# Spectral filter and expert layer on one core: another order for the opening loads, for the rest of the first transform, and for the turned loads ahead of the input loads

## The chip, the cores and the metric

The kernel runs on one core of one Trainium2 chip. The metric is the device time of one execution in microseconds (us), as the median of several; lower is better. The profiled execution is a single one, recorded by the hardware profiler, and it took somewhat longer than the runs that are only timed (the table below has both).

## The reference, cut to what matters

```python
def _attn_ref(x, w_r, w_i, b_r, b_i):              # x: (8, 2496, 256)
    X = np.fft.rfft(x, axis=1)
    Xr, Xi = X.real, X.imag
    Yr = Xr @ w_r - Xi @ w_i + b_r
    Yi = Xr @ w_i + Xi @ w_r + b_i
    Yr = np.sign(Yr) * np.maximum(np.abs(Yr) - 0.01, 0.0)
    Yi = np.sign(Yi) * np.maximum(np.abs(Yi) - 0.01, 0.0)
    return np.fft.irfft(Yr + 1j * Yi, n=2496, axis=1)

def _moe_ref(x, w_gate, w1, w2):                   # x: (19968, 256), 8 experts, hidden 1024
    logits = x @ w_gate
    expert_idx = argmax(logits); gate_w = softmax(logits)[expert_idx]
    for e in range(8):
        out[mask_e] = gate_w[mask_e] * (np.maximum(x[mask_e] @ w1[e], 0) @ w2[e])
```

The first function runs on 8 sequences (batches) of 2496 rows, the second on all 19,968 rows together.

## The kernel before, in words

A transform of length 2496 is done as 39 x 64. For each batch `fwd_a` applies the 39-point step: the input lies in six blocks `x` (q = 0 to 5, each loaded by `load_x`; blocks 0 to 4 are 117 x 1024 values, 468 KB, block 5 is 78 x 512 values, 156 KB), and each block is done in one or two pairs (q, g), 11 pairs a batch. The result of a pair (`pa` in PSUM) is copied to SBUF (`ae`, four buffers that are used in turn; for batch 0 most of it into the large tile `z` instead) and stored to a buffer in DRAM (`spec_dram`). `turn` loads it back turned: a tile `t` for slot s of batch b needs rows 12s to 12s+11 of the stored array and is fetched by two transfers of 128 KB. There are 10 slots a batch. In slot s, `fwd_b` multiplies the tile by a block of the basis `bm` (the 64-point step, result `pb`), `halves` copies and splits the result, `mix` multiplies by the weights (`pk`, `pm`, result `v`), `shrink` thresholds it (`r`, `y`), and two slots later `inv_b` goes back (`pv`) by the basis `bi`. Blocks 12 to 19 of `bi` are loaded, blocks 0 to 11 are made on the chip from `bm` by `turn_basis` (four transposes on TensorE into `pi`, one copy on ScalarE).

The program runs a fixed loop of 80 slots (`it`), and the order on each engine is the order of the code; nothing is reordered. Iteration `it` does `fwd_b` of slot it+1, `inv_b` of slot it-2, `mix` of slot it, and what is listed for it of the next batch's first step: ScalarE rounds a block of x (`round_x`, result `xah`), GpSimd takes the remainder (`rest_x`, result `xal`), TensorE multiplies (`fwd_a`), ScalarE copies `ae`, SyncE stores it. Which pair and which load of x belongs to which iteration stands in two tables of offsets (lines 630 to 635). At the end of an iteration come the rounds for the next-but-one iteration, then the basis loads, the turns and the loads of x (lines 709 to 736).

SyncE (SP) issues nearly all transfers, one after the other. When a transfer must wait for data (a turn for the rows that it reads, a load for a buffer to come free), SP waits, and all that stands behind it waits too. Slot k below is the stretch that begins with `pb` of the k-th slot of the loop; slot 10 is the first of batch 1.

Before the loop stands the opening: batch 0's 11 pairs, a store of rows 0 to 47 in pieces (`store_first`), the first turns, a store of rows 48 to 71 and one of rows 72 to 119 (`store_rest`, three transfers each: pair 0's columns from the tile `first_ae`, which is one of the four `ae` buffers, the rest from `z`), blocks of `bm`, and the first two blocks of batch 1. `keep_warm` puts matmuls without use on TensorE while it would have nothing to do. After the spectral part comes the expert layer, in which TensorE has work without a gap; the change doesn't touch it.

Of the kernel before, what the change touches and what calls it, by code (L numbers as in the profile page):

```python
# [24 lines left out]
D = 256  # L25
# [84 lines left out]
class Kernel:  # L110
# [80 lines left out]
    def open_forward(self, st):  # L191
        tc, nc, nb = self.tc, self.nc, self.nb
        f = self.f = self.pool(st, "f", 1, side="right")
        self.xst = ExitStack()
        self.xp = self.pool(self.xst, "xp", 3)
        self.skip(self.xp, 224)
        self.xh, self.xl = {}, {}
        self.tp = self.pool(st, "tp", 6, side="right")
        self.w = self.pool(st, "w", 2, side="right")
        self.psf = self.pool(st, "psf", 1, side="right", space=PSUM)  # L200

        y = [self.w.tile([128, 2, D], F32, tag="y", name=f"first{i}", bufs=3) for i in range(2)]
        self.idle, self.row1, self.brow = y[0][:, 0, :].bitcast(BF16), y[0][0:1, 1, 0:128], y[1][0:1]
        nc.vector.memset(self.idle, 0.0)
        nc.vector.memset(self.row1, 1.0)
        far = f.tile([117, 240], F32, name="far")
        self.far, self.fer = far[:, 0:120], far[0:78, 120:240]
        nc.sync.dma_start(far, self.c_fa)
        self.bm = f.tile([128, K1, 128], F32, name="bm")
        self.bi = f.tile([128, K1, 128], F32, name="bi")  # L210
        self.bias = f.tile([128, 2, D], F32, name="bias")
        self.bias_r = f.tile([128, 2, D], F32R, name="bias_r")
        self.ones = f.tile([128, 128], F32R, name="ones")
        self.xg = {}
        for z, zf in zip(self.zs, self.zf):
            for c in range(2):
                nc.vector.memset(z[:, c, 64:66, :], 0.0)
            nc.vector.memset(zf[:, 5280:5288], 0.0)
        for q in range(6):
            self.load_x(0, q)  # L220
        raw = self.wi.tile([128, 4, D], F32, tag="yb", name="wraw", bufs=4)
        nc.sync.dma_start(raw, self.w_in.rearrange("(c p) n -> p c n", p=128))
        self.skip(self.wi, 160)
        self.raw = {"r": raw[:, 0:2, :], "i": raw[:, 2:4, :]}
        nc.sync.dma_start(self.brow, self.b_in.rearrange("(o h) n -> o h n", o=1))
        self.wh, self.wl = {}, {}
        for nm in "rds":
            self.wh[nm] = f.tile([128, 2, D], F32R, name="wh" + nm)
            self.wl[nm] = f.tile([128, 2, D], F32R, name="wl" + nm)
        self.nlam = f.tile([128, 1], F32, name="nlam")  # L230
        nc.vector.memset(self.nlam, -LAM)
# [138 lines left out]
    def fwd_a(self, b, q, g):  # L370
        nc = self.nc
        x = self.part_x(b, q, g)
        p = self.psi.tile([128, 512], F32, tag="u", name="pa", bufs=4)
        if b:
            h, l = self.xh.pop((b, q, g)), self.xl.pop((b, q, g))
            fh, fl = self.fhl[q == 5]
            for i, (a, v) in enumerate(((fh, h), (fl, h), (fh, l))):
                nc.tensor.matmul(p[:120, :], a, v, start=i == 0, stop=i == 2)
        else:
            nc.tensor.matmul(p[:120, :], (self.far if q < 5 else self.fer)[:x.shape[0], :], x, start=True, stop=True)  # L380
        n = 2 * q + g // 2 - 1
        if b or n < 0:
            ae = self.xp.tile([120, 2, D], F32, tag="ae", name="ae", bufs=4)
            to = ae.rearrange("p g d -> p (g d)")
        else:
            to = self.zs[1][:120, n // 5, 0:NB, :].rearrange("p n a -> p (n a)")[:, n % 5 * 512:n % 5 * 512 + 512]
            ae = to.rearrange("p (g d) -> p g d", g=2)
        if b == 0 and g:
            nc.vector.tensor_copy(to, p[:120, :])
        else:  # L390
            with self.tc.high_priority():
                nc.scalar.copy(to, p[:120, :])
        if b:
            nc.sync.dma_start(self.spec[b % 2][:, 4 * q + g:4 * q + g + 2, :], ae)
        elif n < 0:
            self.first_ae = ae
# [186 lines left out]
    def spectral(self, fwd):  # L583
# [5 lines left out]
        pairs = [(q, g) for q in range(6) for g in ((0, 2) if q < 5 else (0,))]  # L589
        todo = [(b, s) for b in range(nb) for s in range(10)]  # L590
        n = len(todo)
        self.keep_warm(10)
        nc = self.nc
        for i, pair in enumerate(pairs):
            self.fwd_a(0, *pair)
            if i in (0, 5):
                self.store_first(0, 48, *((-1, 0) if i == 0 else (0, 5)))
            if i == 5:
                self.load_basis(0, 4)
            if i in (8, 10):  # L600
                self.store_first(0, 32, *((5, 8) if i == 8 else (8, 10)))
        self.store_first(32, 48, 5, 10)
        self.turn(0, 0, (0,))
# [7 lines left out]
        self.load_basis(8, 12)  # L611
        if nb > 1:
            self.load_x(1, 1)
        self.store_rest(72, 120)
        self.load_basis(12, 16)
        self.keep_warm(6)
        self.spread_bias()
        self.keep_warm(6)
# [9 lines left out]
        for b in range(1, nb):  # L628
            at = 10 * b - 10
            for i, o in enumerate({1: (2, 2, 3, 3, 4, 4, 5, 5, 6, 6, 7), 2: (-2, -1, 0, 1, 1, 2, 3, 4, 4, 5, 6)}.get(  # L630
                    b, (-3, -2, -1, 0, 1, 2, 3, 3, 4, 5, 6))):
                first[at + o].append((b, *pairs[i]))
            for q, o in enumerate({1: (None, None, 0, 1, 2, 3), 2: (-5, -4, -3, -1, 0, 2)}.get(b, (-7, -5, -4, -2, 0, 2))):
                if o is not None:
                    loads[at + o].append((b, q))
        for b in range(nb):
# [4 lines left out]
        for b in range(nb - 1):  # L641
# [5 lines left out]
            for i in range(GH):  # L647
                o = i + 2 if i < 3 else i + 1
                (late if i == 3 else early)[at + o].append((self.inv_z, b, i))
                o = i + 3 if i < 3 else i + 2  # L650
                to = (late if i == 3 else early)[at + o]
                to.insert(0 if i == 2 else len(to), (self.inv_y, b, i))

        for it in range(n):
            b, s = todo[it]
# [53 lines left out]
            for a in first.get(it + 2, ()):  # L709
                if a[0] > 1:  # L710
                    self.round_x(*a)
            if it == 2:
                self.load_basis(16, 20)
            if it in (2, 4):
                self.turn_basis(it // 2)
            if it in (4, 6):
                self.load_inverse(*((12, 16), (16, 20))[it // 2 - 2])
            if not it:
                self.turn(*todo[4])
                self.turn(*todo[5])  # L720
            elif it < 5:
                self.turn(*todo[it + 5])
            for a in loads[it]:
                self.load_x(*a)
            if it in (2, 8, 9):
                self.load_tables(max(it - 7, 0), self.paced)
            if it == 6:
# [2 lines left out]
                self.split_bias(it - 7)  # L730
            if it == 11:
                self.write_blank(self.us[b, s][0:1, 0, 0:1])
            if 6 < it < n - 4:
                if it == 7:
                    self.turn(*todo[it + 3])
                self.turn(*todo[it + 4])
            if b == nb - 3 and s == 6:
                self.tabling = self.table(0)
            if b == nb - 1 and s == 2:
# [586 lines left out]
```

## Time and profile before

| | us |
|---|---|
| median of 3 timed runs (lowest, highest) | 1443.52 (1442.25, 1444.67) |
| the profiled execution | 1455.2 |
| its span in the trace | 1453.3 |
| TensorE matmuls busy in it | 1429.0 |
| VectorE busy | 926.8 |
| ScalarE busy | 770.1 |

The profiled execution is 1.9 us longer than its span, and 11.7 us longer than the median of the timed runs. Differences are worked out inside the trace and applied to the median.

### The profile page before, as it was taken

The page shows a single profiled execution, that of the slowest core. Times are in us where ns is not written, and L with a number is a line of the kernel's source. Part 1 is how long each engine was busy: PE and PEld are TensorE (multiplying, and loading weights), DVE is VectorE, ACT ScalarE, POOL GpSimd, SP SyncE. Part 2 cuts the span into 40 slices and gives each one's busy share as a digit, 9 for nine tenths or more (in the row PEclk, how much of TensorE's full clock was granted, in tenths as well). Part 3 has the DMA queues.
Part 4 walks back from the last instruction along what each step waited for, and adds up shares of the span by engine and source line. Part 5 has one row for each costly group of instructions (what it writes and reads, how often), then busy time and mean ns, then how long its engine had stood idle before and what let it go on. Part 6 is the DMA issues. An engine that isn't in the chain of part 4 may idle for free. (4 is left out here: it accounts for less than half of the span.)

```text
span 1453.3 us, 35136 instructions
## 1 busy us (share of the span) xinstructions
PE 1429.0 (98%) x10521; PEld 1308.2 (90%) x10522; DVE 926.8 (64%) x1960; ACT 770.1 (53%) x1551; POOL 490.8 (34%) x595
## 2 busy tenths in 40 slices
PE   8999999999999989999999999999999999999998
PEld 5889898898989877899999999999999999999997
DVE  4788898988998875555555545454646445446444
ACT  4878787777877763443444434343435334335332
POOL 0452565766674454334311112112112112112111
PEclk9999999999999999999999999999999999999999
DMA  8774565565554232444343323242324224223220
GB/s 236 238 215 133 145 187 161 162 175 164 166 153 151 71 98 72 118 124 111 92 106 105 102 53 107 48 105 66 86 53 105 49 49 107 53 60 89 49 49 29
DMA packets 193212, 161.34 MB, mean 111 GB/s; under 512 B 127163, under 2 KB 163798, under 8 KB 192788
## 3 DMA queue, kind: packets, MB, share of 16 engines
q1 hardware_dynamic: 173043, 114.63, 31.1%
q0 software_dynamic: 19808, 44.03, 8.7%
q8 instruction: 94, 1.54, 0.5%
q14 instruction: 123, 1.00, 0.2%
q10 hardware_dynamic: 144, 0.13, 0.0%
HBM read 241.22 MB, written 66.37 MB: 212 GB/s over the span
## 5 line engine op out<-in xcount | busy, mean ns | idle before, releaser
L1163 PE MATMUL ph<-xh,l 128*128 128x256 f32 x1312 | 363.0, 277 | 0.2 <-DVE l L1094 0.2
L1163 PE MATMUL ph<-xh,h 128*128 128x256 f32 x1312 | 363.1, 277 | 0.0
L1163 PE MATMUL ph<-xl,h 128*128 128x256 f32 x1312 | 362.9, 277 | 0.0
L1203 PE MATMUL po<-h,hh 128*128 128x512 f32 x1296 | 310.5, 390 | 2.3 <-DVEq L1113 1.5
L1169 DVE SCALAR_TENSOR_TENSOR hl<-ph,hh 128x512 fp32r<-128x512 f32 x328 | 225.5, 688 | 134.7 <-ACT hh L1168 115.0
L1212 POOL DMA_INDIRECT out<-o,row x124 | 123.4, 995 | 551.6 <-DVE o L1210 521.3
L1168 ACT ACTIVATE hh<-ph 128x512 fp32r<-128x512 f32 x328 | 194.8, 600 | 189.0 <-PE ph L1163 160.6
L1203 PEld LDWEIGHTS po<-h,hh 128*128 128x128 f32 x1296 | 236.5, 188 | 48.9 <-ACTq L1105 2.9
L1210 DVE SCALAR_TENSOR_TENSOR o<-po,xr,part 128x256 f32<-128x256 f32 x156 | 74.0, 483 | 278.5 <-ACT part L1209 245.1
L1163 PEld LDWEIGHTS ph<-xh,l 128*128 128x128 f32 x1312 | 246.3, 188 | 0.6 <-DVE l L1094 0.4
L1163 PEld LDWEIGHTS ph<-xh,h 128*128 128x128 f32 x1312 | 246.3, 188 | 0.5 <-ACT yb L543 0.3
L1163 PEld LDWEIGHTS ph<-xl,h 128*128 128x128 f32 x1312 | 246.6, 188 | 0.0
L1209 ACT ACTIVATE part<-po,xr 128x256 f32<-128x256 f32 x156 | 72.3, 474 | 312.6 <-PE po L1205 279.0
L892 POOL DMA_INDIRECT xs_dram<-yb,pos x176 | 178.5, 1014 | 59.6 <-issue 47.9
L1205 PEld LDWEIGHTS po<-h,hl 128*128 128x128 f32 x1296 | 165.1, 188 | 6.9
L1205 PE MATMUL po<-h,hl 128*128 128x256 f32 x1296 | 167.3, 279 | 0.0
L483 DVE SCALAR_TENSOR_TENSOR y<-v,r 64x256 f32<-64x256 f32 x320 | 134.1, 419 | 5.8 <-ACT r L477 0.6
L366 POOL TENSOR_TENSOR xal<-x,xah 117x512 fp32r<-117x512 f32 (+1 forms) x77 | 97.4, 1270 | 0.2 <-issue 0.2
L831 POOL COPY mark<-y 1x1 f32<-1x1 f32 x77 | 27.4, 356 | 203.9 <-DVE y L483 168.7
L503 ACT COPY z<-pv 128x256 f32<-128x256 f32 x160 | 94.0, 709 | 0.5 <-PE py L536 0.5
L416 PE MATMUL pb<-bm,t 128*128 128x128 f32 x640 | 87.7, 280 | 6.0 <-DMA t<-spec_dram 6.0
L416 PEld LDWEIGHTS pb<-bm,t 128*128 128x128 f32 x640 | 79.0, 193 | 15.9 <-issue 9.9
(205 smaller groups left out, 2474.1 us busy)
## 6 DMA issues: line engine op xcount, KB each, us to landing
r<-moe_w SPq DMA_DIRECT2D x672, 128.0 KB
r<-moe_w SPq DMA_DIRECT2D x166, 512.0 KB
xq<-xs_dram SPq DMA_DIRECT2D x332, 64.0 KB
t<-spec_dram SPq DMA_DIRECT2D x159, 128.0 KB
spec_dram<-ae SPq DMA_DIRECT2D x77, 240.0 KB
x<-x SPq DMA_DIRECT2D x38, 468.0 KB
xs_dram<-yb,pos POOLq DMA_INDIRECT x176
xs_dram<-blank POOLq DMA_DIRECT2D x8, 264.0 KB
```

What stands on the lines that cost most here:

```text
L366: i = self.paced = self.nc.gpsimd.tensor_sub(l, x, self.xh[b, q, g])
L416: nc.tensor.matmul(p[:, c, :, kp, :], t[:, kp, c * 128:(c + 1) * 128], self.bm[:, 2 * s + kp, :], start=True, stop=True)
L483: nc.vector.scalar_tensor_tensor(out=y[q * 64:q * 64 + 64, kp, :], in0=u[h, q, :], scalar=LAM, in1=r[h, q, :], op0=ALU.add, op1=ALU.min)
L503: nc.scalar.copy(self.zs[b % 2][:, c, 0:NB, 4 * s:4 * s + 4].rearrange("p n a -> p a n"), p[:, c].rearrange("p a r n -> p (a r) n"))
L892: i = nc.gpsimd.indirect_dma_start(out=self.xs[:, :], out_offset=bass.IndirectOffsetOnAxis(ap=pos[:n, g:g + 1], axis=0), in_=y[:n, g, :], ...
L1163: nc.tensor.matmul(p[:, i, :], a[:, c, f * 128:(f + 1) * 128], v[:, c, :], start=m == 0, stop=m == 5)
L1168: nc.scalar.activation(hh[:, s, :], p, AF.Relu)
L1169: nc.vector.scalar_tensor_tensor(out=hl[:, s, :], in0=p, scalar=0.0, in1=hh[:, s, :], op0=ALU.max, op1=ALU.subtract)
L1203: nc.tensor.matmul(p, hh[:, f, hs], w2[:, f].rearrange("p a d -> p (a d)"), start=f == 0, stop=False)
L1205: nc.tensor.matmul(p[:, :D], hl[:, f, hs], w2[:, f, 0, :], start=False, stop=f == 7)
L1210: nc.vector.scalar_tensor_tensor(out=o[:, h, :], in0=p[:, :D], scalar=xr[:, h, 0:1], in1=part, op0=ALU.mult, op1=ALU.add)
L1212: i = nc.gpsimd.indirect_dma_start(out=self.out[:, :], out_offset=bass.IndirectOffsetOnAxis(ap=at[h], axis=0), in_=o[:, h, :], in_offset=N ...
```

## The change

1. In the opening the small block (q = 5) of x is loaded first, and its pair is the first of the 11. The last copy, that of pair (4, 2), is shared by ScalarE and VectorE. The last piece of the store of rows 0 to 31 goes out after the new last pair.
2. The store of rows 72 to 119 and the load of blocks 12 to 15 of `bm` leave the opening. Rows 72 to 95 are stored at the end of iteration 0, behind a load of x, rows 96 to 119 at the end of iteration 2. Blocks 12 to 15 of `bm` are loaded in iteration 2, blocks 16 to 19 in iteration 4 (before: 2). Blocks 12 to 15 of `bi` are loaded in iteration 5 (before: 4), blocks 16 to 19 in iteration 7 (before: 6), behind the turns.
3. From iteration 7 on the turns are issued ahead of the loads of x of the same iteration.
4. Blocks 4 to 7 of `bi` are made in iteration 1 (before: 2).
5. Blocks 1 and 2 of x of batch 2 are loaded one iteration later (7 and 8).

```diff
-        for q in range(6):
+        for q in (5, 0, 1, 2, 3, 4):
             self.load_x(0, q)
...
-        if b == 0 and g:
+        if (b, q, g) == (0, 4, 2):
+            nc.scalar.copy(to[:, :D], p[:120, :D])
+            nc.vector.tensor_copy(to[:, D:], p[:120, D:])
+        elif b == 0 and g:
             nc.vector.tensor_copy(to, p[:120, :])
...
-        for i, pair in enumerate(pairs):
-            self.fwd_a(0, *pair)
+        for i in (10, *range(10)):
+            self.fwd_a(0, *pairs[i])
...
-            if i in (8, 10):
+            if i in (8, 9):
                 self.store_first(0, 32, *((5, 8) if i == 8 else (8, 10)))
...
-        self.store_rest(72, 120)
-        self.load_basis(12, 16)
...
-            for q, o in enumerate({1: (None, None, 0, 1, 2, 3), 2: (-5, -4, -3, -1, 0, 2)}.get(b, (-7, -5, -4, -2, 0, 2))):
+            for q, o in enumerate({1: (None, None, 0, 1, 2, 3), 2: (-5, -3, -2, -1, 0, 2)}.get(b, (-7, -5, -4, -2, 0, 2))):
...
-            if it == 2:
-                self.load_basis(16, 20)
+            if it in (1, 4):
+                self.turn_basis(1 + it // 4)
             if it in (2, 4):
-                self.turn_basis(it // 2)
-            if it in (4, 6):
-                self.load_inverse(*((12, 16), (16, 20))[it // 2 - 2])
+                self.load_basis(*((12, 16), (16, 20))[it // 2 - 1])
+            if it == 5:
+                self.load_inverse(12, 16)
...
+            if 6 < it < n - 4:
+                if it == 7:
+                    self.turn(*todo[it + 3])
+                self.turn(*todo[it + 4])
+            if it == 7:
+                self.load_inverse(16, 20)
             for a in loads[it]:
                 self.load_x(*a)
+            if it in (0, 2):
+                self.store_rest(*((72, 96), (96, 120))[it // 2])
...
-            if 6 < it < n - 4:
-                if it == 7:
-                    self.turn(*todo[it + 3])
-                self.turn(*todo[it + 4])
```

The first place is SP's list from the second block of x of batch 1 (the last load of the opening) to the load of x in iteration 2. A turn is two transfers, so a row `x2` is one slot's tile; before the change:

```order
L337 DMA x<-x 117x1024
L246 DMA spec_dram<-ae 48x512
L246 DMA spec_dram<-z_104 48x2560 x2
L257 DMA bm<-c_bm 128x512
L403 DMA t_341<-spec_dram 64x2x256 x2
L403 DMA t_344<-spec_dram 64x2x256 x2
L337 DMA x<-x 117x1024
L403 DMA t_404<-spec_dram 64x2x256 x2
L337 DMA x<-x 117x1024
L394 DMA spec_dram<-ae 120x512 x2
L257 DMA bm<-c_bm 128x512
```

and in the change, where `t_338`, `t_341` and `t_410` are the tiles of slots 4, 5 and 6:

```order
L337 DMA x<-x 117x1024
L406 DMA t_338<-spec_dram 64x2x256 x2
L406 DMA t_341<-spec_dram 64x2x256 x2
L337 DMA x<-x 117x1024
L246 DMA spec_dram<-ae 24x512
L246 DMA spec_dram<-z_104 24x2560 x2
L406 DMA t_410<-spec_dram 64x2x256 x2
L337 DMA x<-x 117x1024
L397 DMA spec_dram<-ae 120x512 x2
L257 DMA bm<-c_bm 128x512
```

The turns of slots 4 and 5 now stand right behind the load of x, without 1056 KB of stores and 256 KB of basis ahead of them. The turn of slot 6 stands right behind the store of the rows that it reads, and behind it a load of x and slot 3's two stores of `ae`.

The second place is SP's list in iterations 6 and 7; before the change:

```order
L260 DMA bi<-c_bi 128x512
L337 DMA x<-x 117x1024
L394 DMA spec_dram<-ae 120x512
L337 DMA x<-x 117x1024
L403 DMA t_896<-spec_dram 64x2x256 x2
L403 DMA t_899<-spec_dram 64x2x256 x2
L394 DMA spec_dram<-ae 120x512
```

and in the change, where the first load of x is block 0 of batch 2, the last one block 1, and `t_894` and `t_897` are the tiles of slots 10 and 11 (the first two of batch 1):

```order
L337 DMA x<-x 117x1024
L397 DMA spec_dram<-ae 120x512 x3
L406 DMA t_894<-spec_dram 64x2x256 x2
L406 DMA t_897<-spec_dram 64x2x256 x2
L260 DMA bi<-c_bi 128x512
L337 DMA x<-x 117x1024
L397 DMA spec_dram<-ae 120x512
```

Block 1 of x of batch 2, before the change the load ahead of the last store of batch 1, now stands behind that store, four transfers of turns and a basis block.

## Rows read from the trace of the kernel before

**Rows 1.** Busy us by stretch: PE, PEld, DVE, ACT, POOL (instructions), granted clock, DMA share, GB/s.
```profile
25.00:57.00 32.00, 28.67 (x204) 26.31 (x203) 22.68 (x48) 22.50 (x48) 13.27 (x15) 0.95 0.91 268
...
41.40:44.90 3.50, 3.45 (x17) 3.48 (x17) 0.42 (x2) 1.31 (x3) 1.70 (x3) 0.51 0.88 239
...
100.00:300.00 200.00, 200.00 (x1562) 180.28 (x1561) 174.85 (x402) 158.59 (x343) 107.88 (x128) 1.00 0.56 162
```

**Rows 2.** What TensorE waited for from 16 to 110: total, times, longest.
```profile
PE pb L416 <- DMA t<-spec_dram: 6.0, 4, 2.4
```

**Rows 3.** TensorE's timeline, slots 3 to 5: start, duration, idle before and its releaser.
```profile
34.19 0.71 PE L499 MATMUL pv<-bi,y 128*128 128x128 f32 x4 [0.65 <-DVE y L483]
...
38.48 0.60 PE L266 MATMUL pi<-ident,bm 128*128 128x128 f32 x4
41.45 2.05 PE L416 MATMUL pb<-bm,t 128*128 128x128 f32 x8 [2.38 <-DMA t<-spec_dram]
...
48.41 1.05 PE L416 MATMUL pb<-bm,t 128*128 128x128 f32 x8
...
52.06 0.39 PE L378 MATMUL pa<-xal,fah 117*120 117x512 f32 x1
...
53.66 0.60 PE L266 MATMUL pi<-ident,bm 128*128 128x128 f32 x4
```

**Rows 4.** The same timeline, slots 10 and 11.
```profile
76.10 1.13 PE L416 MATMUL pb<-bm,t 128*128 128x128 f32 x8 [1.89 <-DMA t<-spec_dram]
...
81.64 1.08 PE L499 MATMUL pv<-bi,y 128*128 128x128 f32 x8
```

**Rows 5.** SP's timeline, 25 to 44: when each group of transfers was issued.
```profile
25.30 0.55 SPq L246 DMA_DIRECT2D spec_dram<-ae  x1
...
33.97 5.23 SPq L403 DMA_DIRECT2D t<-spec_dram  x4
...
39.92 1.22 SPq L403 DMA_DIRECT2D t<-spec_dram  x2
41.23 0.52 SPq L337 DMA_DIRECT2D x<-x  x1
```

**Rows 6.** SP's timeline in slots 8 and 9.
```profile
64.69 0.39 SPq L260 DMA_DIRECT2D bi<-c_bi  x1
...
69.11 0.32 SPq L394 DMA_DIRECT2D spec_dram<-ae  x1
69.53 0.34 SPq L337 DMA_DIRECT2D x<-x  x1
72.68 2.54 SPq L403 DMA_DIRECT2D t<-spec_dram  x4
```

**Rows 7.** ScalarE's and GpSimd's timelines in slot 5.
```profile
52.19 1.09 ACT L392 COPY ae<-pa 120x512 f32<-120x512 f32 x2
53.14 1.18 ACT L359 CAST xah<-x 117x512 fp32r<-117x512 f32 x2
...
54.19 2.51 POOL L366 TENSOR_TENSOR xal<-x,xah 117x512 fp32r<-117x512 f32 x2
```

**Rows 8.** ScalarE's timeline, slots 8 to 10, and one row of VectorE's.
```profile
68.49 0.59 ACT L392 COPY ae<-pa 120x512 f32<-120x512 f32 x1
...
73.79 0.62 ACT L359 CAST xah<-x 117x512 fp32r<-117x512 f32 x1
74.44 0.62 ACT L314 CAST bh<-bias 1x512 fp32r<-1x512 f32 x1
77.32 0.37 ACT L427 COPY re<-pb 128x256 f32<-128x256 f32 x1 [2.27 <-PE pb L416]
...
81.08 0.87 DVE L483 SCALAR_TENSOR_TENSOR y<-v,r 64x256 f32<-64x256 f32 x2
```

**Rows 9.** The opening: ScalarE's last copy of the first step, and TensorE's wait.
```profile
16.15 0.59 ACT L392 COPY z<-pa 120x512 f32<-120x512 f32 x1 [1.13 <-PE pa L380]
...
22.96 1.13 PE L416 MATMUL pb<-bm,t 128*128 128x128 f32 x8 [1.14 <-DMA t<-spec_dram]
```

## The prediction

> **What bounds the kernel now.** I read the busy times by stretch first. From 100 to 300 us TensorE is busy 200.00 of 200.00 us at full clock [rows 1], and it goes on so through the expert layer: time is lost only where TensorE waits, and what it loses early it never gets back. Between 25 and 57 us it is busy 28.67 of 32.00, while the DMA engines are at 0.91 of their time and move 268 GB/s [rows 1]: that is the stretch in which the change moves transfers. Next, the list of waits: from 16 to 110 us TensorE waited four times for a turned tile, 6.0 us together, 2.4 the longest [rows 2]. The timeline places them: 2.38 before slot 4's `pb` at 41.45 [rows 3], 1.89 before slot 10's at 76.10 [rows 4], the rest in the opening [rows 9]. The longest costs more than itself: `pb` then takes 2.05 us where slot 5's takes 1.05 [rows 3], and the granted clock is 0.51 between 41.40 and 44.90 [rows 1], the lower of the two levels (1.2 GHz). Behind the 1.89 us wait `pb` takes 1.13 [rows 4], so the clock stayed up there.
>
> **Gain A: slot 4's wait.** Its tile was issued at 33.97 [rows 5], behind 1056 KB of stores and 256 KB of basis. Now it stands right behind the second block of x. To place landings I use an estimate in bytes: from the store of rows 48 to 71 (issued 25.30 [rows 5]) to slot 4's tile SP's list held 528 + 256 + 468 + 1056 + 256 + 256 KB = 2.89 MB, 10.8 us at 268 GB/s; the tile was there at 41.45, 16.15 us later, so some 5.4 us of backlog and latency lay ahead. In the new list it is 1.54 MB, 5.8 us: landed at about 25.3 + 5.4 + 5.8 = 36.5, ahead of the 38.48 at which TensorE is free. The four transposes at 38.48 [rows 3] move to iteration 1, where slot 3's `pv` waits 0.65 for `y` anyway [rows 3]; if that cover were gone they would cost up to 0.60. So `pb` of slot 4 starts at 38.48 instead of 41.45: 2.97. Slot 4 took 48.41 - 41.45 = 6.96 at half clock, slot 5 up to its transposes 53.66 - 48.41 = 5.25 [rows 3]: 1.71 more. **A = -4.7**, and slot 5 would start at 43.7.
>
> **Loss B: a buffer of `ae`.** There are four. `first_ae` held one until its rows were stored, in a transfer listed ahead of the loop; now it is held until the end of iteration 2. So the second `ae` copy of slot 4 has to take the buffer of slot 3's first, and waits until that one's store has landed. Behind that copy stand ScalarE's rounds of x for slot 5. The store stands on SP behind slot 6's tile, which waits for rows 72 to 95 to land. By the same estimate these are 528 + 256 + 468 + 512 + 468 + 528 KB = 2.83 MB after 25.3, landed at 25.3 + 5.4 + 10.5 = 41.2. Then two issues of a turn, 1.22, and one of x, 0.52 [rows 5]: the store goes out at 43.0. Such a store's landing is not a row of its own; one issued at 69.11 let the turn that waits for it go at 72.68 [rows 6], 3.6 later with a load of x right behind it. Less than 3.6 by what 468 KB take at 268 GB/s (1.7) is 1.9. Landing is then between 44.9 and 46.6; I take 46.0, near the upper end, since half a megabyte of turn and x is just ahead of it. Behind the landing: the copy and the first round, each half of a pair's time (0.55 and 0.59), and both remainders on GpSimd, 2.51 [rows 7], some 3.6 together, so TensorE's last product of the pair is at 49.6. Unhindered it would be 3.65 after slot 5's `pb` (52.06 - 48.41 [rows 3]), at 47.4. **B = +2.2**, from +1.1 to +2.8 by the landing, and nothing if the list drains 2.2 us sooner than I estimate. The wait is in pieces, with products between, so I leave the clock up.
>
> **Loss C: block 1 of x of batch 2.** In slot 9 ScalarE's list is: `ae`, the round of that block (`xah`), `bh`, and then `re`, the first copy of slot 10's `pb`. Before the change the block had been loaded in iteration 6. Now its load stands on SP behind slot 8's `ae` store, the turns of slots 10 and 11, which wait for that store's landing, and a block of `bi`. Counted from the end of slot 8's `ae` copy (68.49 + 0.59 = 69.08 [rows 8]): the store goes out at 69.11, lands after 2.5 (between 1.9 and 3.6 as above; no x stands right behind it any more) at 71.6; four issues of turns take 2.54 and one of `bi` 0.39 [rows 6], so the load goes out at 74.6. Its time has no row. Two bounds: slot 10's tile was complete at 76.10 [rows 4], of which the second half can't have been issued before 72.68 + 0.64, so 128 KB took at most 2.8; and with 724 KB of `bi` and x at 268 GB/s on top it would be 5.5. I take 4.6, nearer the upper end, as there is more data: landed at 79.2. Then `xah` and `bh`, 0.65 + 0.62 [rows 8], and `re` at 80.5, against 77.32 [rows 8]. **C = +3.15**, from +0.75 (1.9 and 2.8) to +5.1 (3.6 and 5.5). That passes on: `re` leads by ScalarE and VectorE to `y`, whose last half ended at 81.08 + 0.87 = 81.95 [rows 8], while the `pv` that needs it began its first half at 81.64 [rows 4]; there was no slack. The 1.89 us wait for slot 10's tile gets shorter by some 1.0, but that lies inside C. TensorE then stands still for over 2 us in a row ahead of slot 11's `pb`, as before slot 4; I add 0.4 for the clock (nothing to 1.7, a part of it beside VectorE).
>
> By the Trainium skill (DMA: Bandwidth & Descriptors, Anatomy of one DMA), whose fit for one transfer is 2.0 us and its bytes at 436 GB/s, the load of x would be an estimated 3.1 us and C 1.5 less; the sum would then be -0.4 instead of +1.1. No row has a block of x alone, so the trace can't decide it.
>
> **The rest.** The opening: TensorE begins behind `keep_warm` and does 11 pairs as before. The store of 48 rows goes out one pair later, and the last copy (0.59, [rows 9]) is halved to some 0.4. Behind both is a wait of 1.14 for slot 0's tile [rows 9]: between -0.2 (the copy) and +0.9 (one pair), taken as nothing, since the last piece of the store sets that tile. The order of turns and x from iteration 8 on, the later blocks of `bm` and `bi` (`bm` 12 to 15 is needed at slot 6, `bi` 16 to 19 at the `pv` of 81.64 [rows 4]) and block 2 of x each have several us to spare in slots where TensorE waits for nothing.
>
> **Sum.** -4.7 + 2.2 + 3.15 + 0.4 = +1.1. The profiled execution would go from 1455.2 to 1456.3; the median from 1443.5 to **1444.6**. Within 0.2% is 1440.6 to 1446.4; less can't be told from no change here.
>
> **The rivals.**
> - *Only C.* The stores drain sooner, B is nothing. For it: the DMA engines are busy only 0.91 [rows 1], and a tile lands at 36.5 only if they keep up. -4.7 + 3.15 + 0.4 = -1.1: 1442.4 (1440 to 1444.5). Chance 0.20.
> - *Neither: faster.* B is nothing and C at its lower end, which takes a store that lands in 1.9 and a load of x in 2.8: -4.7 + 0.75 = -3.9, 1439.6, and 1438.8 if the opening gains too. It decides once C stays below 1.8. Against it: x can't be issued before the store of slot 8 has landed and five transfers are out. Chance 0.17.
> - *The clock falls too: slower.* The two stalls are as long as the one that is removed; if TensorE drops to the lower level after each, as it did at 41.45, that costs 1.7 apiece instead of 0.4 in all: -4.7 + 2.2 + 3.15 + 3.4 = +4.1, 1447.6, up to 1450 with the upper ends of C. It decides above +2.9. Chance 0.20. For it: the 2.38 us wait did it; against it: 1.89 did not, and B is in pieces.
> - *The forecast:* A, B and C as worked out, 1441.5 to 1447.5. Chance 0.43; a twelfth of that on the faster side, a quarter on the slower.
>
> **Numbers.** Faster: 0.04 + 0.05 (only C) + 0.15 = 0.24. Slower: 0.11 + 0.16 = 0.27. Within: 0.49. Leaving out a tenth at either end gives 1439.5 to 1449.0.
>
> **What the profile after would show.** A: no wait for `t` at slot 4, `pb` there 1.05 to 1.15 us long, clock 1.00 from 38 to 45. B: a wait of ScalarE's second `ae` copy in slot 4 for a store, and of TensorE for `xal` in slot 5. C: a wait of ScalarE's `xah` for x in slot 9, `re` over 11 us after slot 8's `ae` copy (8.24 before), TensorE waiting ahead of slot 11. Slots after 12 shifted by the sum, all alike. The prediction is wrong if SP isn't held where I say: if slot 6's tile goes out well ahead of 41, B is gone; if block 1 of x goes out ahead of 73, C is.

## The result: 0.9% slower

| | kernel before | the change |
|---|---|---|
| median of the timed runs, us | 1443.97 (6 runs, 1441.74 to 1445.87) | 1456.43 (6 runs, 1454.77 to 1457.87) |
| ratio, 95% interval | | 1.0088 (1.0075 to 1.0101) |
| profiled execution, us | 1455.2 | 1456.57 |

The change costs 12.5 us; a time between 1439.5 and 1449.0 had been forecast, most likely 1444.6. The runs of this study fell on chips on which the kernel before takes 1443 or 1452 us, the difference lying mostly between 450 and 565 us, which the change doesn't touch, and its first profile has the slower stretch; so times are compared as ratios on one chip, and traces by their first 100 us.

The waits of TensorE from 16 to 110 us in the profile after (total, times, longest) answer to [rows 2]:

```profile
PE pa L378 <- ACT xah L359: 4.9, 1, 4.9
PE pb L419 <- ACT r L480: 4.9, 1, 4.9
PE pb L419 <- DMA t<-spec_dram: 2.2, 2, 1.2
...
```

The waits for a turned tile are down from 6.0 to 2.2 us. Two new ones of 4.9 us each stand in their place, both for ScalarE. TensorE's timeline after, with the rows that answer to [rows 3, 4]:

```profile
39.79 1.05 PE L419 MATMUL pb<-bm,t 128*128 128x128 f32 x8
45.09 1.05 PE L419 MATMUL pb<-bm,t 128*128 128x128 f32 x8
...
52.64 0.78 PE L378 MATMUL pa<-xah,fah 117*120 117x512 f32 x1 [4.91 <-ACT xah L359]
58.71 1.06 PE L419 MATMUL pb<-bm,t 128*128 128x128 f32 x8
...
80.37 1.13 PE L419 MATMUL pb<-bm,t 128*128 128x128 f32 x8 [1.22 <-DMA t<-spec_dram]
90.06 2.05 PE L419 MATMUL pb<-bm,t 128*128 128x128 f32 x8 [4.90 <-ACT r L480]
97.42 1.05 PE L419 MATMUL pb<-bm,t 128*128 128x128 f32 x8
```

Slot 4 (39.79) begins without a wait, at full speed, and takes 5.30 us: gain A is there. In slot 5 TensorE stands 4.91 us before the first product of a pair, and slot 6 begins at 58.71 instead of 54.10. Ahead of slot 11 (90.06) it stands 4.90 us, and slot 12 begins at 97.42 instead of 85.33, 12.1 us late. From there on to 440 us the shift stays at 11 to 12 us.

What held ScalarE is in its own timeline:

```profile
43.58 0.59 ACT L395 COPY ae<-pa 120x512 f32<-120x512 f32 x1
51.49 0.58 ACT L395 COPY ae<-pa 120x512 f32<-120x512 f32 x1 [7.32 <-DMA spec_dram<-ae]
51.97 1.14 ACT L359 CAST xah<-x 117x512 fp32r<-117x512 f32 x2
...
73.62 0.59 ACT L395 COPY ae<-pa 120x512 f32<-120x512 f32 x1
...
86.76 0.62 ACT L359 CAST xah<-x 117x512 fp32r<-117x512 f32 x1 [7.92 <-DMA x<-x]
87.40 0.62 ACT L314 CAST bh<-bias 1x512 fp32r<-1x512 f32 x1
88.05 0.37 ACT L430 COPY re<-pb 128x256 f32<-128x256 f32 x1
```

The second `ae` copy of slot 4 waits 7.32 us for a store, and the rounds of x (`xah`) that slot 5 needs stand behind it: loss B. The `xah` at 86.76 waits 7.92 us for a load of x, with `bh` and slot 10's `re` behind it: loss C. Why both transfers were late is on SP:

```profile
37.58 0.37 SPq L246 DMA_DIRECT2D spec_dram<-ae  x1
38.00 0.79 SPq L246 DMA_DIRECT2D spec_dram<-z  x2
43.79 1.23 SPq L406 DMA_DIRECT2D t<-spec_dram  x2
45.12 0.50 SPq L337 DMA_DIRECT2D x<-x  x1
45.73 0.78 SPq L397 DMA_DIRECT2D spec_dram<-ae  x2
...
74.24 0.32 SPq L397 DMA_DIRECT2D spec_dram<-ae  x1
76.82 2.54 SPq L406 DMA_DIRECT2D t<-spec_dram  x4
79.41 0.60 SPq L260 DMA_DIRECT2D bi<-c_bi  x1
80.05 0.39 SPq L337 DMA_DIRECT2D x<-x  x1
```

SP stores rows 72 to 95 until 38.79 and then issues nothing for 5 us: slot 6's tile must wait for those rows to land. The store that ScalarE needs goes out at 45.73, though its copy had been done at about 39, and lands 5.7 us later. In the second place SP stands from 74.56 to 76.82 for the turns, and block 1 of x goes out at 80.05, 5.8 us after the store, and is there at 86.7. The busy times by stretch (columns as in [rows 1]):

```profile
38.00:45.00 7.00, 7.00 (x54) 6.62 (x54) 5.75 (x13) 5.44 (x12) 4.70 (x6) 1.00 0.59 177
52.50:58.70 6.20, 5.91 (x22) 4.64 (x23) 3.86 (x9) 5.26 (x12) 3.90 (x4) 0.55 0.67 238
89.90:97.50 7.60, 7.44 (x38) 7.21 (x39) 6.54 (x15) 6.57 (x15) 2.65 (x4) 0.62 0.50 141
25.00:57.00 32.00, 25.55 (x174) 22.33 (x173) 20.47 (x44) 19.73 (x44) 10.51 (x12) 0.91 0.77 227
```

While SP stands, the DMA engines fall to 0.59 of their time (38 to 45 us), and over 25 to 57 us they move 227 GB/s, 268 before. So the transfers didn't go out late for want of bandwidth; SP hadn't issued them. Once it goes on, what had waited goes out close together: from 45.7 to 51.5 us, while the store lands, the engines are at 0.95 and move 279 GB/s, and from 80.0 to 86.7, while block 1 of x does, at 0.82 and 238 GB/s. Each loss thus has two parts, a late issue and a long time to landing. Behind both stalls the granted clock is 0.55 and 0.62.

### The profile page after: what moved, and what is told of

It is laid out like the page before. It is cut to its first block, busy times and chain, and to the rows that moved or that the text cites. A ratio compares the mean times of both kernels' runs of the same rounds, so it can differ in the third digit from the quotient of the medians.

```text
span 1454.8 us, 35135 instructions
## 1 busy us (share of the span) xinstructions
PE 1429.9 (98%) x10521; PEld 1310.8 (90%) x10522; DVE 930.4 (64%) x1960; ACT 780.4 (54%) x1552; POOL 487.7 (34%) x595
## 5 line engine op out<-in xcount | busy, mean ns | idle before, releaser
L1215 DVE SCALAR_TENSOR_TENSOR o<-po,xr,part 128x256 f32<-128x256 f32 x156 | 74.2, 484 | 286.5 <-ACT part L1214 254.2
```

What stands on the lines that cost most here:

```text
L1215: nc.vector.scalar_tensor_tensor(out=o[:, h, :], in0=p[:, :D], scalar=xr[:, h, 0:1], in1=part, op0=ALU.mult, op1=ALU.add)
```

## The experiments

Starts of `pb` in each trace (us), and the timed ratio to the kernel before on the same chip:

| kernel | slot 0 | 4 | 5 | 6 | 10 | 12 | ratio (95%) |
|---|---|---|---|---|---|---|---|
| before | 22.96 | 41.45 | 48.41 | 54.10 | 76.10 | 85.33 | |
| before_again | 22.07 | 41.54 | 48.55 | 54.29 | 75.93 | 85.17 | 1.0002 (0.9990 to 1.0014) |
| after | 24.27 | 39.79 | 45.09 | 58.71 | 80.37 | 97.42 | 1.0088 (1.0075 to 1.0101) |
| after_again | 23.91 | 40.06 | 45.30 | 57.81 | 80.48 | 95.31 | 1.0081 (1.0060 to 1.0103) |
| open_only | 23.81 | 42.16 | 49.11 | 54.80 | 76.43 | 85.67 | 1.0011 (1.0001 to 1.0021) |
| rows_only | 22.50 | 38.07 | 43.38 | 56.96 | 80.24 | 89.47 | 1.0025 (1.0016 to 1.0033) |
| late_x_only | 22.58 | 41.90 | 50.15 | 55.89 | 76.91 | 91.62 | 1.0036 (1.0025 to 1.0046) |
| x_early | 22.95 | 38.47 | 43.78 | 57.16 | 79.81 | 89.22 | 1.0040 (1.0028 to 1.0053) |
| x_ahead | 24.64 | 40.13 | 45.37 | 59.17 | 80.95 | 90.17 | 1.0047 (1.0032 to 1.0063) |
| turn_late | 24.69 | 40.17 | 45.42 | 52.38 | 78.62 | 94.68 | 1.0069 (1.0044 to 1.0095) |
| ae_early | 23.77 | 39.30 | 44.60 | 51.90 | 79.03 | 94.47 | 1.0100 (1.0074 to 1.0125) |
| warm | 24.86 | 40.38 | 45.69 | 58.26 | 82.29 | 98.31 | 1.0073 (1.0052 to 1.0094) |
| turns_late_x_early | 23.62 | 39.15 | 44.45 | 51.34 | 75.08 | 84.31 | 1.0015 (1.0004 to 1.0025) |
| best | 23.23 | 38.73 | 43.97 | 51.38 | 75.06 | 84.61 | 1.0000 (0.9990 to 1.0009) |
| best2 | 22.34 | 37.86 | 43.11 | 48.79 | 71.83 | 81.06 | 0.9985 (0.9976 to 0.9994) |

Slots 0 to 5 show gain A (25.45 us before, 20.82 after), 5 to 6 loss B (5.69, 13.62), 10 to 12 loss C (9.23, 17.05).

**Controls.** The kernel before and the change again, unchanged.

> The kernel before, unchanged, profiled a second time. Its first profile stood 11.7 us above its timed runs and only 1.5 us below the profile of the change, although at 100 us the change was already 11.6 us behind it; the gap closed between 450 and 565 us. Theory: that first profile was a slow draw at the end of the spectral part, and this one has a span near 1442 us with the same first 110 us (waits of 2.4 and 1.9 us for a turned tile). Rival: the profiler lengthens this kernel always, and the change wins some 10 us back at the end of the spectral part; then the span is near 1453 again. Time ratio to before: 1.000.

> The change, unchanged, beside its variants on one chip (the first variants ran on a chip on which the kernel before takes 1452 us, 8 us more than where the change was timed). Theory: ratio to before as measured, 1.0075 to 1.0101, and in the trace slot 12 begins 11 to 12 us later than in the kernel before. Rival: part of the difference was that of the chips or runs; ratio under 1.006.

The kernel before had a span of 1450.9 us on a chip on which its timed runs took 1452.07, so the profiler does not lengthen it, and the slow stretch goes with the chip: both expectations on that point were off. The first 85 us repeat within 0.9 us, with the waits for a turned tile. The change repeats at 1.0081; its trace is 10 us behind at slot 12, not 12, since loss C was 5.6 this time. So a single trace is good to some 2 us at slot 12.

**Blocks 1 and 2 of x early again.**

```diff
...
-2: (-5, -3, -2, -1, 0, 2)}
+2: (-5, -4, -3, -1, 0, 2)}
...
```

> The change with one thing undone: block 1 of x of batch 2 is loaded in iteration 6 again, ahead of the turns (block 2 as before too); the turns stay ahead of x otherwise. Theory: loss C is the stall of 4.9 us ahead of slot 11 and the slow clock behind it, together 7.3 us in the profile; all of it goes, and slot 12 begins some 7.3 us earlier than in the change: 1449.0 us. Rival 1: the clock falls anyway, or the wait moves to slot 10's tile, and only 3 to 5 us go: 1452 us. Rival 2: the load moves the wait to another transfer, since the DMA engines are full: within 1 us of the change, 1456 us.

Slots 10 to 12 took 9.41 us (17.05 in the change): C is gone, and B as large as before (13.38 from slot 5 to 6). The ratio falls to 1.0040, about 0.45% less than the change: the theory's size. Rival 2 is out; rival 1 (3 to 5 us) is by the trace, while the intervals of the times alone would leave room for it.

**The turn of slot 6 later.**

```diff
-            elif it < 5:
+            elif 1 < it < 5:
+                if it == 2:
+                    self.turn(*todo[6])
                 self.turn(*todo[it + 5])
```

> The change with one thing moved: the turn of slot 6, which waits for rows 72 to 95, is issued in iteration 2 behind slot 3's two stores and a basis block, no longer ahead of them. Theory: loss B comes from SP standing in that wait with the store of slot 3 behind it; the store then goes out at its copy (39 us, 45.7 in the change), ScalarE's second copy of slot 4 waits under 2 us for it, TensorE doesn't stop over 2 us, the clock stays up, and slot 6 begins some 7 us earlier: 1449.3 us. Rival 1: the store lands as late because the DMA engines are full, not because SP holds it: under 2 us of gain, 1455 us. Rival 2: slot 6's tile now comes late instead, a wait for a turned tile of some us at slot 6: 1452 us or more.

B itself fell as the theory had it: slot 5 to 6 took 6.96 us. But the gain was not kept. ScalarE's timeline shows the next waits in the row:

```profile
46.46 0.58 ACT L395 COPY ae<-pa 120x512 f32<-120x512 f32 x1 [1.91 <-DMA spec_dram<-ae]
...
53.64 0.59 ACT L395 COPY ae<-pa 120x512 f32<-120x512 f32 x1 [2.43 <-DMA spec_dram<-z]
...
68.69 0.62 ACT L359 CAST xah<-x 117x512 fp32r<-117x512 f32 x1 [4.18 <-DMA x<-x]
```

The third row is block 0 of batch 2. Its load stands on SP behind slot 8's turn, which waits for rows 96 to 119, as slot 6's waits for 72 to 95; in the change that was covered by B: the block was there at 70.3 us, here at 68.7, but ScalarE came for it so late that it waited only 0.9 us. Slots 6 to 10 took 26.24 us, 22.00 before. Neither the theory nor a rival named this wait.

**first_ae free early.**

```diff
         self.store_rest(48, 72)
+        self.store_first(72, 120, -1, 0)
...
-                self.store_rest(*((72, 96), (96, 120))[it // 2])
+                for part in ((0, 5), (5, 10)):
+                    self.store_first(*((72, 96), (96, 120))[it // 2], *part)
```

> The change with one thing undone: the part of rows 72 to 119 that lies in first_ae (96 KB) is stored ahead of the loop again, so that tile is free early; the parts in z keep their new places. Theory: the second copy of slot 4 then takes that buffer and waits for nothing, but the first copy of slot 5 needs the buffer whose store stands behind slot 6's turn, and waits for its landing at some 51 instead of 49: the loss of 7.9 us at slot 6 shrinks to 2 to 4 us, and the clock may still fall: 1451 us. Rival: with a buffer more the store's delay is covered wholly, as in the kernel before: 1448.5 us.

The 7 us wait of ScalarE's copy in slot 4 is gone, and a wait of 0.71 us in slot 5 is what is left of it, so it was the buffer of `first_ae`. Slot 5 to 6 took 7.30. As in the run before, the next load was late instead (block 0 of batch 2, slots 6 to 10 in 27.13 us, there at 69.1 us), and the timed ratio, 1.0100, is no better than the change's. Both expectations were off: taking one wait away only uncovers the next.

**TensorE kept busy in the two stalls.** The 36 products write a tile that nothing reads.

```diff
+            if it == 10:
+                self.warm_gap(36)
             if it + 1 < n:
                 self.fwd_b(*todo[it + 1])
...
+            if it == 4:
+                self.warm_gap(36)
             for a in first[it]:
                 self.fwd_a(*a)
```

> The change, and in the two long waits of TensorE (before the pairs of slot 5, and before slot 11's pb) 36 products each of 128 x 256 in bf16 whose result nothing reads, some 4 us, so that it isn't idle there. The waits stay as they are. Theory: the clock falls because TensorE stood idle; it stays at its upper level behind both, and some 2 us come back at each: slot 12 begins 3 to 5 us earlier than in the change. Rival: the time behind the waits is lost to late copies on ScalarE and VectorE anyway, or the clock falls all the same: within 1 us of the change.

```profile
48.17 4.10 PE L785 MATMUL pw<-ident 128*128 128x256 bf16 x36
53.50 0.50 PE L378 MATMUL pa<-xah,fah 117*120 117x512 f32 x1 [1.23 <-ACT xah L359]
...
58.26 1.06 PE L419 MATMUL pb<-bm,t 128*128 128x128 f32 x8
```

The clock stays up (granted 1.00 from 53.4 to 58.3 us): the product behind the wait takes 0.50 us where it took 0.78, and from there to slot 6 it is 4.76 us, 6.07 in the change. In the second place slot 11 takes 6.00 us, 7.36 in the change. But the ratio is 1.0073 against 1.0081, no difference that these runs can tell. The rows of ScalarE say where it went:

```profile
72.22 0.62 ACT L359 CAST xah<-x 117x512 fp32r<-117x512 f32 x1 [3.28 <-DMA x<-x]
89.00 0.62 ACT L359 CAST xah<-x 117x512 fp32r<-117x512 f32 x1 [8.21 <-DMA x<-x]
```

These waits were 0.87 and 7.92 us in the change: the next loads land no sooner when TensorE gets on. The half clock costs 1.3 and 1.4 us, if nothing else is late, and here something is. The rival's result holds, by a late load of x and not by a fallen clock.

**Each part alone on the kernel before.** `open_only` has the first four pieces of the change's diff, `late_x_only` the new offsets and the turns ahead of the loads of x (the basis block stays where it was), `rows_only` parts 2 and 4, with that basis block.

> The kernel before with part 1 of the change alone (the opening). Theory: the small block stands ahead of the one that TensorE needs next, the others land 1 to 2 us later, and slot 0 begins 0.5 to 1.5 us later: ratio 1.0004 to 1.001. Rival: no difference, the opening's later start in the runs of the change was scatter: ratio 1.000 and slot 0 within 0.4 us.

> The kernel before with parts 3 and 5 of the change alone: from iteration 7 on the turns ahead of the loads of x, and blocks 1 and 2 of x of batch 2 an iteration later. All else is as before, so no delay comes from the opening or from the stores. Theory: loss C stands by itself; ScalarE waits 4 to 6 us for block 1 in slot 9, slot 12 begins 5 to 6.5 us later than in the kernel before, ratio 1.0035 to 1.0045. Rival: C came only of SP being late already (the waits of loss B behind it); then it is the 3 us of the prediction or less, ratio under 1.0025.

> The kernel before with parts 2 and 4 of the change alone: rows 72 to 95 and 96 to 119 stored at the end of iterations 0 and 2, the basis blocks later, blocks 4 to 7 of bi made in iteration 1; opening, loads of x and their order are as before. Theory: the change is the sum of three parts that each lose time; the opening alone cost 0.11% and the late block of x 0.36% of a total of 0.85%, so gain A and loss B together lose 0.3 to 0.5%, ratio 1.003 to 1.005, slot 6 begins 3 to 5 us later in the trace. Rival: without the opening's delay the store lands in time, the prediction's sum of A and B (a gain of 2.5 us) holds, and the parts only lose together: ratio 0.998 to 1.0005.

They cost 0.11, 0.36 and 0.25%, together 0.72 of the change's 0.81 to 0.88. The opening: slot 0 began on average at 24.06 in the nine traces with the new one and at 22.61 in the six without, 1.4 us. That is the theory's size, but its reason (later blocks of x) covers at most 0.6 us of it, by which TensorE's last pair ended later (16.7 against 16.1); the wait for slot 0's tile was 0.8 us longer too (1.6 against 0.8), and why isn't shown. The late block of x: ScalarE waits 6.00 us for it, and slots 10 to 12 take 14.71, with little delay ahead of it (slot 10 began 0.8 us late), so C stands alone:

```profile
81.68 0.62 ACT L359 CAST xah<-x 117x512 fp32r<-117x512 f32 x1 [6.00 <-DMA x<-x]
```

The stores and basis blocks: gain A is whole (slots 0 to 5 in 20.88 us), loss B too (5 to 6 in 13.58), and slot 12 begins 4.1 us late; ScalarE's copy waits as long as in the change, though the opening is the old one and the store that it needs goes out 2.9 us sooner (42.81, in the change 45.73):

```profile
40.87 1.23 SPq L403 DMA_DIRECT2D t<-spec_dram  x2
42.20 0.50 SPq L337 DMA_DIRECT2D x<-x  x1
42.81 0.78 SPq L394 DMA_DIRECT2D spec_dram<-ae  x2
...
49.60 0.59 ACT L392 COPY ae<-pa 120x512 f32<-120x512 f32 x1 [7.15 <-DMA spec_dram<-ae]
```

The store landed 6.8 us after it went out. The rivals of all three are out, the opening's by little (its interval begins at 1.0001). The stores cost a little less than their theory had it: 1.0025, with slot 6 2.9 us late.

**Order or iteration.** The loads of x ahead of the turns again; block 1 stays an iteration later.

```diff
+            for a in loads[it]:
+                self.load_x(*a)
             if 6 < it < n - 4:
                 if it == 7:
                     self.turn(*todo[it + 3])
                 self.turn(*todo[it + 4])
             if it == 7:
                 self.load_inverse(16, 20)
-            for a in loads[it]:
-                self.load_x(*a)
```

> The change with part 3 undone: the loads of x stand ahead of the turns of the same iteration again, in iteration 7 also ahead of the basis block; block 1 of x of batch 2 stays an iteration later. Theory: it is the order behind the turns that makes C, as they wait for a store's landing: block 1 goes out 5 us earlier, ScalarE's wait falls under 2 us, slot 12 begins 4 to 6 us earlier than in the change, ratio 1.004 to 1.006. Rival: the iteration is what counts, and the load lands too late in either order: under 2 us of gain, ratio 1.007 or more.

Slots 10 to 12 took 9.22 us, as in the kernel before. So C is made by the order behind the turns; the later iteration alone costs nothing there.

**Against all the waits of SP.** Three kernels, each on top of the one before it. The first:

```diff
-2: (-5, -3, -2, -1, 0, 2)}
+2: (-5, -4, -3, -1, 0, 2)}
...
-            elif it < 5:
+            elif it in (2, 4):
+                self.turn(*todo[it + 4])
                 self.turn(*todo[it + 5])
```

> The change with three waits taken away from SP's list: the turns of slots 6 and 7 go out in iteration 2 and those of slots 8 and 9 in iteration 4, each behind that iteration's two stores (the change: one slot in each of iterations 1 to 4), and block 1 of x of batch 2 is loaded in iteration 6 again. Undoing one of these alone gave back 2.6 (turn of slot 6) or 6.3 us (block 1) at slot 12 in the trace, and behind the first a new wait of ScalarE for block 0 of batch 2 stood in slot 8. Theory: all three come from SP standing in a turn's wait with loads and stores behind it; now gain A is left with the opening's 1 us: slot 12 begins 2 to 4 us earlier than in the kernel before, ratio 0.997 to 1.000. Rival: the DMA engines are full up to 57 us, and the waits only change their place: slot 12 at least 3 us later than before, ratio 1.002 or more.

The second puts the opening of the kernel before back:

> The kernel of the run with late turns and the early block 1, and the opening of the kernel before (small block last, its pair last, one engine for the last copy). Theory: the change's opening costs 1 to 1.5 us, because the small block stands ahead of the first that TensorE needs and every other block lands later; slot 12 another 1 to 1.5 us earlier, the fastest of all, ratio 0.996 to 0.999. Rival: the opening's difference is scatter from run to run, no difference to that run within 0.5 us.

With late turns and the early block 1 slot 12 begins 1.0 us ahead of the kernel before, yet the ratio is 1.0015, between theory and rival. With the old opening it is 1.0000, though slot 12 began no earlier in that trace (84.61), so the 1.4 us of the opening aren't shown a second time in a trace. The change's loss is gone, and gain A has been eaten by shorter waits of the same kind (ScalarE waited 2.32 and 2.65 us for `ae` buffers, 1.32 and 1.72 for blocks of x). The last one sets out to take these away, in several places at once:

```diff
...
             if it in (0, 2):
-                self.store_rest(*((72, 96), (96, 120))[it // 2])
+                if not it:
+                    self.store_first(72, 120, -1, 0)
+                for part in ((0, 5), (5, 10)):
+                    self.store_first(*((72, 96), (96, 120))[it // 2], *part)
...
-2: (-5, -4, -3, -1, 0, 2)}
+2: (-6, -4, -3, -1, 0, 2)}
...
-            if 6 < it < n - 4:
-                if it == 7:
-                    self.turn(*todo[it + 3])
+            if 7 < it < n - 4:
                 self.turn(*todo[it + 4])
             if it == 7:
-                self.load_inverse(16, 20)
+                self.turn(*todo[it + 3])
             for a in loads[it]:
                 self.load_x(*a)
+            if it == 7:
+                self.turn(*todo[it + 4])
+                self.load_inverse(16, 20)
```

> The kernel of the run named best, against its four waits that are left: all of first_ae's rows 72 to 119 stored at the end of iteration 0 (so its buffer is free for slot 4's second copy), block 0 of x of batch 2 loaded in iteration 4, and in iteration 7 the order turn of slot 10, x, turn of slot 11, basis block. Theory: the waits of 2.3 and 2.7 us for ae buffers, 1.3 us for block 0 and 1.7 us for block 2 go, and most of gain A is left: slot 12 begins 2 to 4 us earlier than in the kernel before, ratio 0.997 to 0.9985. Rival: the DMA engines are full up to 57 us, the waits only change their place: ratio 0.9995 to 1.001.

0.9985 (0.9976 to 0.9994), 1442.33 us against 1443.85: faster than both kernels. Slots 4 to 7 take 5.3 to 5.7 us each, slot 12 begins at 81.06, 4.3 us ahead. About half of that arrives in the time (0.15%, some 2 us); where the rest goes isn't shown. The stretches 38 to 45 and 25 to 57 us show what changed:

```profile
25.00:57.00 32.00, 31.01 (x236) 28.90 (x237) 26.33 (x56) 26.64 (x58) 15.69 (x18) 1.00 0.87 265
38.00:45.00 7.00, 7.00 (x58) 6.71 (x57) 5.18 (x11) 5.84 (x14) 6.25 (x9) 1.00 0.92 285
```

TensorE is busy 31.01 of 32 us at full clock (25.55 in the change, 28.67 before), and the DMA engines are at 0.92 where they were at 0.59. Over 25 to 57 us they move 265 GB/s, about as much as in the kernel before (268), in an order in which less has to wait. The rival, that the engines are full and a wait can only move, falls here.

## Why the prediction was wrong

- **Gain A** was right in mechanism and size: -4.7 forecast, -4.6 measured (slots 0 to 5, 25.45 to 20.82).
- **Loss B** was the right wait in the right place, and mis-sized: +2.2 forecast, with +2.8 as its upper bound, +7.9 measured. The step that failed is "Landing is then between 44.9 and 46.6; I take 46.0", 3.0 us after the store's issue and at most 3.6. rows_only shows it by itself: there slot 5 began at 43.38 (43.7 forecast) and the store went out at 42.81 (43.0 forecast), and it landed 6.8 us later. In the change it went out at 45.73 (2.7 later than forecast, 1.3 of it by the opening, the rest by a later landing of rows 72 to 95) and landed 5.7 us later. The upper bound was a row from 69 us, with one load of x behind the store and the DMA engines at 0.75 of their time (69.1 to 72.7 us). The store here shared them with a load of x, a second store, a basis block and turns, and they were at 0.95. From the landing to slot 6 it was 7.2 us, 5.6 by the forecast's steps; 1.3 of that is the clock.
- **Loss C** likewise: 3.15 and 0.4 for the clock forecast, 5.5 to 7.8 measured in the six traces that have it (slots 10 to 12, less 9.23). Steps up to the issue held: store to turn 2.58 (2.5), four turns 2.54 (2.54), the basis block 0.60 (0.39). The step that failed is "I take 4.6", with 5.5 as the upper bound: the load took 6.7 us. From the `ae` copy's end (74.21) to `re` (88.05) it was 13.8 us, 11.4 forecast and 8.24 before. That is 5.60 of the 7.82; 0.86 comes of counting from slot 10, which began that much sooner behind the copy, and 1.36 lies behind `re`: from there to slot 12 it was 9.37 us, 8.01 before and 8.02 in warm, where the clock stayed up.
- **The clock** fell behind both stalls, as the slower rival had it (0.55 and 0.62). "The wait is in pieces, with products between, so I leave the clock up" failed: TensorE stood once, for 4.91 us and for `xah`, not for `xal`. The price is 1.3 and 1.4 us, where 0.4 had been taken in all, but it can't be won back alone: warm kept the clock up and gained nothing that can be told, since the next load was late.
- **The opening** was taken as nothing, with +0.9 as the upper end; it costs 1.4 us in the traces and 0.11% in time. "TensorE does 11 pairs as before" failed by 0.6 us, and slot 0's tile was waited for 0.8 us longer.
- **The price on the Trainium skill's page** (DMA: Bandwidth & Descriptors, Anatomy of one DMA), an estimated 3.1 us for a block of x, would have moved the forecast further off: the load took 6.7 us with other transfers around it. The page fits it to single transfers that GpSimd issues; these are issued by SP. The measurement decides.
- **A third wait** of the same kind, block 0 of batch 2 behind slot 8's turn, was missed: the prediction names neither. In the change it is hidden behind B and shows only when B is taken away.

By the traces the sum is +1.3 (opening) - 4.6 (A) + 7.9 (B) - 0.3 (slots 6 to 10) + 7.8 (C) = +12.1 at slot 12, and 12.5 us was timed; in the change's second trace it is 10.0, with 12.9 timed. The forecast had the same two losses at +5.75, not +15.7. That SP standing in a turn's wait, with unrelated stores and loads behind it, makes the losses is shown by turn_late for B and by x_ahead for C, where only a place in SP's list changes and the loss goes (but for 1.3 us of B); that other kernels can do without the waits, by best2. That the landings took so long because the engines were shared is read from their busy shares, and no run tests it by itself. Why the same opening scatters by up to 1.9 us from trace to trace is open as well.

## What to carry to other kernels

- SP issues in order, so a transfer that waits for a landing delays everything listed behind it: put it as late as its user allows, behind the stores and loads that wait for nothing. With four turns moved behind stores and two blocks of x loaded an iteration earlier, the ratio fell from 1.0081 to 1.0015 on one chip; the rest up to 0.9985 took the old opening and a few smaller moves.
- The time from issue to landing belongs to the stretch, not to the transfer: bound it by rows from a stretch that is as full. The 240 KB store took 2.6, 3.6 and 5.7 us here, with the DMA engines at 0.36, 0.75 and 0.95 of their time.
- When one wait goes, ask which wait it covered. Three of the runs here (turn_late, ae_early, warm) removed a stall or its price and won little or nothing.

## What the runs showed of the hardware

- A store of 240 KB took 4.7 to 6.8 us to land in the six traces that have loss B, and a load of 468 KB 5.5 to 7.0 us in the six that have loss C, with other transfers queued around them. With little else in flight (engines at 0.36 of their time, 74.2 to 76.8 us in the change) the turn that waited for such a store went 2.58 us after it.
- After 4.9 us without work TensorE came back at about half clock, and stayed there for most of 6 and 7 us (granted 0.55 and 0.62); after 1.22 and 1.89 us it did not fall. 36 small products in the gap kept it up (1.00).
- The same kernel took 1443 us on two chips and 1452 on two others. The traces differ mostly behind 450 us, in a part of the program that no kernel here changes: from there to 575 us TensorE's waits add up to 2.2 to 2.8 us in the traces from the former and 6.5 to 8.6 in those from the latter.
